# Weight loads in 4,096-byte pieces, rounding in place, and a third group of prepared weights in a fused attention, gated and leaky feed-forward kernel

## The chip, the cores and the metric

One core of a Trainium2 chip runs the whole program. The metric is the device time of one execution in microseconds (us). The kernel before has a median of 1567.53 us over 3 runs (1563.97 to 1570.9). The execution that the profiler recorded took 1571.51 us, 1569.7 us of it from the first to the last instruction.

## The reference, cut to what matters

```python
def sm_attn(qq, kk, vv):
    s = scale * np.matmul(qq, kk.transpose(0, 1, 3, 2))
    s = s - np.max(s, axis=-1, keepdims=True)
    a = np.exp(s)
    return np.matmul(a / (np.sum(a, axis=-1, keepdims=True) + 1e-09), vv)
p_packed = sm_attn(p, k, v)             # 32 packed rows per head
out = sm_attn(q, p_packed, p_packed)    # 8 batches, 8 heads, 576 tokens, 64 wide
x = out.transpose(0, 2, 1, 3).reshape(4608, 512)
x = (1 / (1 + np.exp(-(x @ w_gate))) * (x @ w_val)) @ w_out     # 512 -> 1536 -> 512
h = x @ w_in                                                    # 512 -> 2048
return (np.maximum(0.01 * h, h) @ w_out2).astype(np.float32)    # 2048 -> 512
```

The five weight matrices are float64 (8 bytes a number); q, k, v and p are float32.

## The kernel before, in words

The work has two stages that share the core's memory one after the other.

**The gated stage** goes batch by batch (8 batches of 576 tokens). `attention(b)` makes the two softmaxes of a batch. The second one has only 32 packed rows to look at, so the kernel never forms the attention output: for each group `i` of 256 gate and 256 value columns, `m_mm(i)` (L653) multiplies the packed rows by the weights into a small matrix. ScalarE (ACT) casts it to a high part `mh` and VectorE (DVE) takes the low part `ml` (L673, L676). `mm(f, g)` (L681) then multiplies `mh` and `ml` by the softmax `Ah`, `Al` for gate (g = 0) and value (g = 1) of 128 columns, ACT takes the sigmoid (`sg`, L702), DVE multiplies (L708), and the result is stored to `g1d` in device memory (L713). A batch has 6 groups `i` and 12 blocks `f`, the stage 96 sigmoids.

**The second stage** (`block`, L759) computes the three plain matrix products for 768 tokens at a time with a seven-product scheme (L852). It reads the gated result back (`rawg`, L925) and prepared weights (`wu`, L767).

**Weights.** `unit` (L217) turns 512 float64 numbers per partition into float32, rounded. A load takes both 32-bit words of each number into `raw64` (4 buffers). `scale` (ACT, L228) and `shift` and `sign` (DVE, L235, L239) build the float32 from the high word in a tile `cvs`; `low` (ACT, L231) makes the correction from the low word in `cvf`; `total` (GpSimd, POOL, L247) adds the two into the target. There are 24 units for gate and value weights, which go to the tiles `wc` and stay there, and 44 for the second stage. `staged` (L280) puts 2 units into a tile `Y`, forms the seven combinations (DVE, L311), splits them into high and low parts in `HL` (ACT L317, POOL L323) and stores them (L331) in device memory. There are 22 such groups, with 2 tiles `Y` and 2 tiles `HL`.

**Order.** All of this is a list of tasks with an engine, an assumed cost, a rank, the tasks that must come first, and places taken from pools of buffers. `Plan.run` (L55) simulates the list and writes the instructions in the order that it finds; each engine then runs its own instructions strictly in that order. The queue of the sync engine (SP) issues nearly all loads and the `g1d` stores, POOL issues the stores of prepared weights and the `rawg` loads.

**Handover.** The left memory of the gated stage (`raw64`, `Y`, `HL` and so on) is given up in `open_left`, which stands behind every unit and every stored group (L1059). The right memory (`sg`, `Ah`, `wc` and so on) is given up in `open_right`, which stands behind the last DVE product of the gated stage (L1060); that task also issues the last `g1d` store. `rawg` and `wu` tiles lie on the left, operand tiles `op` on the right:

```python
opened_left = add("", 0, 0, open_left, sum([*stored.values(), *units], []))
opened_right = add("", 0, 0, open_right, [glu_end[B - 1]])
```

Of the kernel before, what the change touches and what calls it, by code (L numbers as in the profile page):

```python
# [17 lines left out]
P = 128  # L18
# [114 lines left out]
def pack_attention_glu_lrelu(  # L133
# [67 lines left out]
    wc = [early.tile([P, NJ, 2, 256], F32, name=f"wc{i}") for i in range(NF1 // 2)]  # L201
# [12 lines left out]
    for name, n in (("raw64", 4), ("cv", 3), ("Y", 2), ("HL", 2)):  # L214
        plan.pool(name, n)

    def unit(key, rank, load, target, after=(), give=(), loads=1):  # L217

        t = {}

        def do_load():
            t["raw"] = stage.tile([P, 512, 2], I32, tag="raw64", bufs=4, name="raw64")
            load(t["raw"])

        def scale():
            t["s"] = stage.tile([P, 512], F32, tag="cvs", bufs=3, name="cvs")
            t["f"] = stage.tile([P, 512], I32, tag="cvf", bufs=3, name="cvf")
            nc.scalar.activation(t["s"], t["raw"][:, :, 1].bitcast(F32), AF.Copy, scale=2.0 ** -112)  # L228

        def low():  # L230
            nc.scalar.activation(t["f"], t["raw"][:, :, 0].bitcast(U32), AF.Copy, scale=2.0 ** -29)  # L231

        def shift():
            s = t["s"].bitcast(I32)
            nc.vector.tensor_single_scalar(s, s, 3, op=ALU.logical_shift_left)  # L235

        def sign():
            s = t["s"].bitcast(I32)
            nc.vector.scalar_tensor_tensor(  # L239
                out=s, in0=t["raw"][:, :, 1], scalar=-(1 << 31), in1=s,  # L240
                op0=ALU.bitwise_and, op1=ALU.bitwise_or,
            )

        def total():
            x = target().bitcast(I32)
            n = x.shape[1]
            nc.gpsimd.tensor_tensor(  # L247
                out=x,
                in0=t["s"].bitcast(I32).rearrange("p (a b) -> p a b", a=n),
                in1=t["f"].rearrange("p (a b) -> p a b", a=n),  # L250
                op=ALU.add,
            )
# [27 lines left out]
    def staged(st, g, kk, rank):  # L280
# [365 lines left out]
    def gated(b, units):  # L646
# [6 lines left out]
        def m_mm(i):  # L653
            def fn():
                ps = ps_pair()
                for j in range(NJ):
                    for hh in range(2):
# [4 lines left out]
                            wc[i][r, j].rearrange("p g c -> p (g c)"),  # L662
# [54 lines left out]
        for i in range(NF1 // 2):  # L717
            m = add("PE", 1.2, r0 + 16 * i - 95, m_mm(i), [packed[b], *units[i]], take=[K("misc", i), K("mhl", i)],
# [322 lines left out]
    with tc.manual_schedule():  # L1041
# [5 lines left out]
        units = [[unit_gv(i, g, jh) for g in range(2) for jh in range(2)] for i in range(NF1 // 2)]  # L1047
# [45 lines left out]
```

## Time and profile before

| | us |
|---|---|
| median of 3 runs (lowest, highest) | 1567.53 (1563.97, 1570.9) |
| the profiled execution | 1571.51 |
| its span, first to last instruction | 1569.7 |
| TensorE (PE) busy | 1426.4 (91%) |
| VectorE (DVE) busy | 1082.0 (69%) |
| ScalarE (ACT) busy | 768.0 (49%) |
| GpSimd (POOL) busy | 437.7 (28%) |
| all 16 DMA engines, hardware queue | 67.3% of the span |

Times in the profile count from the first instruction. In rows, `out<-in` names the tile written and the tiles read, L and a number is a line of the kernel, and what stands behind `<-` in square brackets or after "waited for" is what ended an engine's wait. PE is the engine to watch: where it is idle, the end of the program moves.

### The profile page before, as it was taken

Reading aid. Unit: us, or ns where it says so; the run is one execution under the profiler, and the core shown is the slowest. Engines: PE = TensorE matmul, PEld = TensorE weight load, DVE = VectorE, ACT = ScalarE, POOL = GpSimd, SP = SyncE. Lnnn points to the kernel's source line nnn. Section 1 sums busy time; section 2 is a strip of 40 time slices with the busy share of each in tenths; the row PEclk is TensorE's granted clock in tenths of the full one; section 3 lists DMA queues with packets and bytes.
Section 4 is the critical chain, followed back from the end, with each engine's and each line's share of the span. In section 5 each row is a group of like instructions: output and inputs, shape, how many; then the busy total and the mean of one; then the engine's idle time right before and its main releaser. Section 6 shows DMA issues by size and latency. Waiting matters only on the chain.

```text
span 1569.7 us, 26707 instructions
## 1 busy us (share of the span) xinstructions
PE 1426.4 (91%) x10368; PEld 1336.0 (85%) x10368; DVE 1082.0 (69%) x1438; ACT 768.0 (49%) x1017; POOL 437.7 (28%) x514
## 2 busy tenths in 40 slices
PE   4687989998889828999999999999999999999995
PEld 1565777876768718999999999999999999999995
DVE  5787878967877627668566865687558755885491
ACT  4476666756565524454345433554355434543450
POOL 1332343314345652001710160026001620130006
PEclk8898999999999959999999999999999999999998
DMA  9994686776566879888998899889988898898884
GB/s 227 255 249 153 224 302 221 251 248 213 189 232 228 293 272 355 295 253 264 324 331 254 261 336 320 252 263 319 334 253 264 288 364 257 256 290 253 253 255 120
DMA packets 143070, 414.92 MB, mean 264 GB/s; under 512 B 24544, under 2 KB 35552, under 8 KB 142944
## 3 DMA queue, kind: packets, MB, share of 16 engines
q1 hardware_dynamic: 115744, 335.07, 67.3%
q0 software_dynamic: 27200, 78.14, 14.5%
q8 instruction: 83, 1.36, 0.4%
q14 instruction: 43, 0.35, 0.1%
HBM read 335.02 MB, written 78.12 MB: 263 GB/s over the span
## 4 chain that ended last, share of the span: by engine, by line
PE 70%; DMA 12%; DVE 7%; ACT 4%; POOL 3%; issue 3%; SPq 0%; POOLq 0%; ACTq 0%; DVEq 0%
PE ps_pair L852 60%; PE ps_pair L692 8%; DMA wd<-HL 2%; DMA raw<-in_moe_w_gate_dram 2%; DMA raw<-in_moe_w_out_dram 2%; DMA wu<-HL 1%; DVE Y L311 1%; DMA v<-in_v_dram 1%; POOL out_dram L1027 1%; POOL HL L323 1%; DVE ml L676 1%; DMA rawg<-g1d 1%; PE ps_pair L659 1%; POOL Y L247 1%; DVE cvs L235 1%
## 5 line engine op out<-in xcount | busy, mean ns | idle before, releaser
L852 PE MATMUL ps_pair<-op,wu 128*128 128x384 f32 x5544 | 965.7, 337 | 39.5 <-DMA wu<-wp 33.5
L852 PEld LDWEIGHTS ps_pair<-op,wu 128*128 128x128 f32 x5544 | 963.6, 189 | 41.5 <-ACT op L795 33.5
L1027 POOL DMA_DIRECT2D out_dram<-os x256 | 150.3, 595 | 618.8 <-DVE os L1014 609.5
L795 ACT CAST op<-rawg 128x768 fp32r<-128x768 f32 x168 | 138.3, 835 | 245.3 <-DVE rawg L786 121.3
L692 PE MATMUL ps_pair<-Ah,ml 128*128 128x288 f32 x768 | 181.1, 318 | 52.8 <-DVE ml L676 22.5
L800 DVE TENSOR_TENSOR op<-rawg,op 128x768 fp32r<-128x768 f32 x168 | 158.3, 951 | 87.3 <-ACT op L795 86.1
L692 PEld LDWEIGHTS ps_pair<-Ah,ml 128*128 128x128 f32 x768 | 126.9, 197 | 101.9 <-ACT sg L702 27.6
L869 DVE TENSOR_TENSOR tmp<-ps_pair,tmp 128x768 f32<-128x768 f32 x72 | 68.8, 956 | 154.4 <-PE ps_pair L852 106.0
L692 PE MATMUL ps_pair<-Al,mh 128*128 128x288 f32 x768 | 169.9, 303 | 0.3 <-DVE Al L581 0.2
L692 PE MATMUL ps_pair<-Ah,mh 128*128 128x288 f32 x768 | 169.0, 302 | 0.0
L795 ACT CAST op<-G 128x768 fp32r<-128x768 f32 x168 | 134.7, 834 | 59.8 <-PE ps_pair L852 44.8
L800 DVE TENSOR_TENSOR op<-G,op 128x768 fp32r<-128x768 f32 x168 | 155.7, 948 | 7.7 <-ACT op L795 7.3
L323 POOL TENSOR_TENSOR HL<-Y,HL 128x1024 fp32r<-128x1024 f32 (+1 forms) x44 | 94.7, 2155 | 129.7 <-ACT HL L317 128.3
L692 PEld LDWEIGHTS ps_pair<-Al,mh 128*128 128x128 f32 x768 | 128.6, 196 | 0.9 <-DVE Al L581 0.9
L692 PEld LDWEIGHTS ps_pair<-Ah,mh 128*128 128x128 f32 x768 | 127.8, 195 | 0.0
L925 POOL DMA_DIRECT2D rawg<-g1d x96 | 68.0, 712 | 160.7 <-ACT op L795 66.6
L988 ACT ACTIVATE G<-G 128x768 f32<-128x768 f32 x96 | 81.2, 846 | 59.0 <-DVE G L985 58.0
L247 POOL TENSOR_TENSOR Y<-cvs,cvf 128x512 int32<-128x512 int32 x44 | 58.5, 1334 | 149.2 <-DVE cvs L239 104.8
L863 ACT COPY tmp<-ps_pair 128x768 f32<-128x768 f32 x72 | 57.5, 799 | 84.5 <-PE ps_pair L852 84.0
L786 DVE TENSOR_TENSOR rawg<-rawg 128x768 f32<-128x768 f32 x96 | 90.2, 952 | 4.1 <-DMA rawg<-g1d 3.3
L786 DVE TENSOR_TENSOR G<-G 128x768 f32<-128x768 f32 x96 | 91.1, 950 | 0.3
L708 DVE TENSOR_TENSOR sg<-sg,ps_pair 128x576 f32<-128x576 f32 x96 | 71.5, 744 | 28.0 <-ACT sg L702 11.2
(75 smaller groups left out, 1147.3 us busy)
## 6 DMA issues: line engine op xcount, KB each, us to landing
wu<-wu SPq DMA_DIRECT2D x168, 512.0 KB, 4.6
wu<-wd SPq DMA_DIRECT2D x168, 512.0 KB, 4.5
wu<-wp SPq DMA_DIRECT2D x126, 512.0 KB, 5.0
g1d<-sg SPq DMA_DIRECT2D x96, 288.0 KB, 4.0
rawg<-g1d POOLq DMA_DIRECT2D x48, 384.0 KB, 8.7
raw<-in_moe_w_out_dram SPq DMA_DIRECT2D x28, 512.0 KB, 6.8
raw<-in_k_dram SPq DMA_DIRECT2D x16, 576.0 KB, 5.1
raw<-in_q_dram SPq DMA_DIRECT2D x16, 576.0 KB, 6.2
```

The lines of the kernel that those rows point to most:

```text
L247: nc.gpsimd.tensor_tensor(out=x, in0=t["s"].bitcast(I32).rearrange("p (a b) -> p a b", a=n), in1=t["f"].rearrange("p (a b) -> p a b", a=n) ...
L323: nc.gpsimd.tensor_tensor(out=hl[:, :, 1], in0=t["y"][:, x0:x1], in1=hl[:, :, 0].bitcast(F32), op=ALU.subtract,)
L692: nc.tensor.matmul(ps[:, t, :HS], w, x[:, t * HS:(t + 1) * HS], start=(n == 0), stop=(n == len(pairs) - 1),)
L708: nc.vector.tensor_tensor(out=sg, in0=sg, in1=st["gv", f, 1][:, :, :HS], op=ALU.mult)
L786: nc.vector.tensor_tensor(out=src(g, o), in0=src(g, a), in1=src(g, b), op=ALU.subtract)
L795: nc.scalar.copy(h, src(g, c))
L800: (nc.gpsimd if on_pool(i, g) else nc.vector).tensor_tensor(out=l, in0=src(g, c), in1=tiles["op", st, i, g][0].bitcast(F32), op=ALU.subtract)
L852: nc.tensor.matmul(ps[c][:, m, :TB], a, x[:, kk, :], start=(fresh and kk == 0 and y == 0), stop=(end and kk == 1 and y == 2), skip_group_c ...
L869: nc.vector.tensor_tensor(out=T[x], in0=ps[c][:, :, :TB], in1=T[y], op=ALU.add)
L925: nc.gpsimd.dma_start(out=t[:, :, t0 - base:t0 - base + m], in_=g1d[b][:, f:f + 2, s0:s0 + m])
L988: nc.scalar.activation(dest(), dest(), AF.Prelu, alpha=0.01)
L1027: nc.gpsimd.dma_start(out=ob[:, s0:s0 + m, d0:d0 + 32], in_=tiles["os", c][32 * y:32 * y + 32, x, t0:t0 + m],)
```

## The change

It has five parts:

- a gate or value unit is now 512 neighbouring columns of one pair of 64-row strips, instead of 256 columns of two pairs: each row that a load reads is one run of 4,096 bytes, before it was two of 2,048. One `wc` tile now holds what two held, and two groups `i` need the same 8 units, before each needed 4 of its own;
- `scale`, `shift` and `sign` work in the target (`wc` or `Y`) itself, and `total` adds `cvf` into it; `cvs` is gone;
- a third `Y` tile;
- a staged unit's load no longer stands behind a free `Y`; its `scale` does;
- the planner's assumed costs of `shift` and `sign` are 0.6 and 0.78 instead of 0.42 and 0.75.

```diff
-    wc = [early.tile([P, NJ, 2, 256], F32, name=f"wc{i}") for i in range(NF1 // 2)]
+    wc = [early.tile([P, NJ, 2, 512], F32, name=f"wc{i}") for i in range(NF1 // 4)]
...
-    for name, n in (("raw64", 4), ("cv", 3), ("Y", 2), ("HL", 2)):
+    for name, n in (("raw64", 4), ("cv", 3), ("Y", 3), ("HL", 2)):
...
         def scale():
-            t["s"] = stage.tile([P, 512], F32, tag="cvs", bufs=3, name="cvs")
+            x = t["x"] = target()
+            nc.scalar.activation(
+                x, t["raw"][:, :, 1].bitcast(F32).rearrange("p (a b) -> p a b", a=x.shape[1]),
+                AF.Copy, scale=2.0 ** -112,
+            )
...
-        L = add("DMA", 1.7, rank, do_load, after, take=[("raw64", ("raw64", key))])
-        a = add("ACT", act(512), rank, scale, [L], take=[("cv", ("cv", key))])
-        c = add("ACT", act(512), rank, low, [a], give=[("raw64", key)])
-        s = add("DVE", 0.42, rank, shift, [a])
-        s = add("DVE", 0.75, rank, sign, [s], give=[("raw64", key)])
-        return add("POOL", gps(512), rank, total, [c, s, *after], give=[("cv", key), *give])
+        L = add("DMA", 1.7, rank, do_load, take=[("raw64", ("raw64", key))])
+        a = add("ACT", act(512), rank, scale, [L, *after])
+        c = add("ACT", act(512), rank, low, [a], take=[("cv", ("cv", key))], give=[("raw64", key)])
+        s = add("DVE", 0.6, rank, shift, [a])
+        s = add("DVE", 0.78, rank, sign, [s], give=[("raw64", key)])
+        return add("POOL", gps(512), rank, total, [c, s], give=[("cv", key), *give])
...
-                r0 = (hh * NJ + 2 * jh) * D
+                r0 = (hh * NJ + j) * D
                 nc.sync.dma_start(
-                    out=raw[64 * hh:64 * hh + 64].rearrange("p (j c) b -> p j (c b)", j=2),
-                    in_=w[r0:r0 + 2 * D, i * 512:(i + 1) * 512].rearrange("(j d) c -> d j c", d=D),
+                    out=raw[64 * hh:64 * hh + 64].rearrange("p c b -> p (c b)"),
+                    in_=w[r0:r0 + D, i * 1024:(i + 1) * 1024],
                 )
...
-            ("gv", i, g, jh), -60 + 4 * i + 2 * g + jh, load,
-            lambda: wc[i][:, 2 * jh:2 * jh + 2, g],
+            ("gv", i, g, j), -60 + 8 * i + 2 * j + g, load, lambda: wc[i][:, j:j + 1, g],
...
-                            wc[i][r, j].rearrange("p g c -> p (g c)"),
+                            wc[i // 2][r, j, :, (i % 2) * 256:(i % 2 + 1) * 256],
...
-            m = add("PE", 1.2, r0 + 16 * i - 95, m_mm(i), [packed[b], *units[i]], take=[K("misc", i), K("mhl", i)],
+            m = add("PE", 1.2, r0 + 16 * i - 95, m_mm(i), [packed[b], *units[i // 2]], take=[K("misc", i), K("mhl", i)],
```

The planner makes another order of it. **First place: ACT at the end of the gated stage**, where `sg` are the last sigmoids, `HL` the casts of prepared weights, `cvs`, `cvf` and `Y<-raw` the rounding of staged units, `op` the first cast of the second stage. Before:

```order
L702 ACTIVATE sg<-ps_pair 128x576 x2
L317 CAST HL<-Y 128x4x256
L317 CAST HL<-Y 128x3x256
L228 ACTIVATE cvs<-raw_6287 128x512
L231 ACTIVATE cvf<-raw_6287 128x512
L228 ACTIVATE cvs<-raw_6298 128x512
L231 ACTIVATE cvf<-raw_6298 128x512
L317 CAST HL<-Y 128x4x256
L317 CAST HL<-Y 128x3x256
L795 CAST op<-rawg 128x768 x11
```

Now:

```order
L315 CAST HL<-Y 128x3x256
L700 ACTIVATE sg<-ps_pair 128x576
L671 CAST mh<-ps_pair 128x1024
L700 ACTIVATE sg<-ps_pair 128x576 x2
L671 CAST mh<-ps_pair 128x1024
L700 ACTIVATE sg<-ps_pair 128x576 x2
L671 CAST mh<-ps_pair 128x1024
L700 ACTIVATE sg<-ps_pair 128x576 x2
L671 CAST mh<-ps_pair 128x1024
L700 ACTIVATE sg<-ps_pair 128x576 x3
L793 CAST op<-rawg 128x768 x6
```

Before, two units and four `HL` casts stand behind the last sigmoid; now the last `HL` cast stands ahead of the last ten sigmoids. **Second place: SP around the same point**, where `raw` are the last loads of staged units, `g1d` the stores of the gated stage, `wu` the first loads of the second stage. Before:

```order
L713 DMA g1d_64<-sg 128x576
L288 DMA raw_6166<-in_moe_w_out_dram 128x1024
L713 DMA g1d_64<-sg 128x576 x3
L288 DMA raw_6287<-in_moe_w_out_dram 128x1024
L713 DMA g1d_64<-sg 128x576
L288 DMA raw_6298<-in_moe_w_out_dram 128x1024
L767 DMA wu<-wp_65 128x1024
```

Now:

```order
L286 DMA raw_5676<-in_moe_w_out_dram 128x1024
L711 DMA g1d_63<-sg 128x576 x4
L711 DMA g1d_64<-sg 128x576 x7
L765 DMA wu<-wp_65 128x1024
L711 DMA g1d_64<-sg 128x576
L765 DMA wu<-wp_66 128x1024
L711 DMA g1d_64<-sg 128x576
L765 DMA wu<-wp_67 128x1024
```

Before, the last staged load stands behind the last `g1d` store and ahead of the first `wu` load; now it stands 16 `g1d` stores ahead of the end, and `wu` loads stand between the last stores. **Third place: ACT at the first group of batch 0**, where `cvs` or `wc` and `cvf` with a `raw` number are the two ACT steps of one gate or value unit, and `w`, `Ah` belong to the second softmax. Before (the fifth to seventh unit are in these rows):

```order
L228 ACTIVATE cvs<-raw_283 128x512
L231 ACTIVATE cvf<-raw_283 128x512
L228 ACTIVATE cvs<-raw_297 128x512
L231 ACTIVATE cvf<-raw_297 128x512
L228 ACTIVATE cvs<-raw_308 128x512
L673 CAST mh<-ps_pair 128x1024
```

Now (the ninth and tenth unit are `raw_410` and `raw_418`):

```order
L577 CAST Ah<-w_389 128x2x288
L577 CAST Ah<-w_393 128x2x288
L234 ACTIVATE cvf<-raw_365 128x512
L227 ACTIVATE wc_94<-raw_410 128x512
L234 ACTIVATE cvf<-raw_410 128x512
L227 ACTIVATE wc_94<-raw_418 128x512
L234 ACTIVATE cvf<-raw_418 128x512
L671 CAST mh<-ps_pair 128x1024 x2
```

The first `mh` cast stood behind seven units and ahead of `Ah`; now two `mh` casts stand together behind ten units and behind `Ah`.

## Rows read from the trace of the kernel before

**Rows 1.** Busy time by stretch; columns are named in the first line.

```profile
core 0: us, PE busy (x) PEld busy (x) DVE busy (x) ACT busy (x) POOL busy (x), PEclk, DMA share, GB/s
44.10:129.30 85.20, 62.65 (x622) 49.62 (x622) 64.47 (x109) 54.55 (x81) 30.17 (x22) 0.86 0.87 226
129.30:546.90 417.60, 381.41 (x3967) 315.47 (x3967) 329.74 (x536) 260.39 (x363) 168.36 (x119) 0.96 0.71 237
...
620.00:1569.70 949.70, 931.67 (x5372) 930.59 (x5370) 624.09 (x697) 409.45 (x509) 199.90 (x326) 0.99 0.86 278
```

**Rows 2.** Chain that ended last, 430 to 600 us: start, us, what.

```profile
565.42 4.71 DMA wd<-HL
...
572.69 6.29 DMA rawg<-g1d
```

**Rows 3.** Timeline at the handover: start, us, engine, line, operation, [idle before <-releaser].

```profile
547.01 0.75 DVE L708 TENSOR_TENSOR sg<-sg,ps_pair 128x576 f32<-128x576 f32 x1 [0.30 <-issue]
...
547.79 0.32 SPq L713 DMA_DIRECT2D g1d<-sg  x1
...
579.28 0.83 ACT L795 CAST op<-rawg 128x768 fp32r<-128x768 f32 x1 [16.77 <-DMA rawg<-g1d]
...
580.16 0.69 PE L852 MATMUL ps_pair<-op,wu 128*128 128x384 f32 x1 [33.25 <-DMA wu<-wp]
...
581.16 7.78 PE L852 MATMUL ps_pair<-op,wu 128*128 128x384 f32 x36 [0.30 <-DVE op L800]
...
591.32 18.83 PE L852 MATMUL ps_pair<-op,wu 128*128 128x384 f32 x107 [2.38 <-DVE op L800]
```

**Rows 4.** Timeline of ACT: the tenth sigmoid from the end, and the last.

```profile
506.13 0.65 ACT L702 ACTIVATE sg<-ps_pair 128x576 f32<-128x576 f32 x1 [1.77 <-PE ps_pair L692]
...
545.36 0.65 ACT L702 ACTIVATE sg<-ps_pair 128x576 f32<-128x576 f32 x1 [2.52 <-PE ps_pair L692]
```

**Rows 5.** The `g1d` stores (L713), 500 to 560 us.

```profile
DMA to landing us min/median/max: 2.7/4.1/6.0
```

**Rows 6.** The `rawg` loads (L925), 540 to 700 us: issue ns, and landing.

```profile
L925 POOL DMA_DIRECT2D rawg<-g1d x30: 704/712/721, 572.7 to 642.6; - x30
...
DMA to landing us min/median/max: 5.3/8.5/12.5
```

**Rows 7.** Timeline of PE in batch 0: first products of groups 1 and 3.

```profile
62.19 0.85 PE L692 MATMUL ps_pair<-Ah,ml 128*128 128x288 f32 x2 [8.22 <-DVE ml L676]
...
89.20 0.53 PE L692 MATMUL ps_pair<-Ah,ml 128*128 128x288 f32 x2 [2.04 <-DVE ml L676]
```

**Rows 8.** Timeline, all engines, start of the gated stage.

```profile
36.18 1.00 ACT L673 CAST mh<-ps_pair 128x1024 fp32r<-128x1024 f32 x1
...
37.47 1.22 DVE L676 TENSOR_TENSOR ml<-ps_pair,mh 128x1024 fp32r<-128x1024 f32 x1
...
44.19 1.42 DVE L581 TENSOR_TENSOR Al<-w,Ah 128x576 fp32r<-128x576 f32 x2
...
48.78 0.66 ACT L228 ACTIVATE cvs<-raw 128x512 f32<-128x512 f32 x1
```

**Rows 9.** DMA, 46 to 97 us: queue, packets, MB, share; issues with median landing.

```profile
q1 hardware_dynamic: 6597, 13.16, 102.1%
...
raw<-in_moe_w_gate_dram SPq DMA_DIRECT2D x14, 256.0 KB, 7.3
```

**Rows 10.** DMA, 120 to 548 us.

```profile
q1 hardware_dynamic: 31932, 63.14, 45.1%
```

**Rows 11.** What ACT waited for, 120 to 548 us: total, times, longest.

```profile
ACT HL L317 <- DVE Y L311: 25.8, 16, 3.6
...
ACT cvs L228 <- DMA raw<-in_moe_w_in_dram: 7.3, 4, 4.6
```

**Rows 12.** Groups of instructions: count, busy us, mean ns.

```profile
L239 DVE SCALAR_TENSOR_TENSOR cvs<-raw,cvs 128x512 int32<-128x512 int32 x68 | 52.6, 783 | 0.9
L235 DVE TENSOR_SCALAR cvs<-cvs 128x512 int32<-128x512 int32 x68 | 42.8, 639 | 27.8 <-ACT cvs L228 27.7
```

More of the change, by code (lines that the diff above doesn't have):

```diff
@@ L225, in scale, with low @@
         def scale():
-            t["s"] = stage.tile([P, 512], F32, tag="cvs", bufs=3, name="cvs")
+            x = t["x"] = target()
[3 more added lines that the diff above has]
+            )
+        def low():
             t["f"] = stage.tile([P, 512], I32, tag="cvf", bufs=3, name="cvf")
-            nc.scalar.activation(t["s"], t["raw"][:, :, 1].bitcast(F32), AF.Copy, scale=2.0 ** -112)
@@ L230, in low @@
-        def low():
             nc.scalar.activation(t["f"], t["raw"][:, :, 0].bitcast(U32), AF.Copy, scale=2.0 ** -29)
         def shift():
-            s = t["s"].bitcast(I32)
-            nc.vector.tensor_single_scalar(s, s, 3, op=ALU.logical_shift_left)
+            x = t["x"].bitcast(I32)
+            nc.vector.tensor_single_scalar(x, x, 3, op=ALU.logical_shift_left)
         def sign():
-            s = t["s"].bitcast(I32)
+            x = t["x"].bitcast(I32)
             nc.vector.scalar_tensor_tensor(
-                out=s, in0=t["raw"][:, :, 1], scalar=-(1 << 31), in1=s,
-                op0=ALU.bitwise_and, op1=ALU.bitwise_or,
+                out=x, in0=t["raw"][:, :, 1].rearrange("p (a b) -> p a b", a=x.shape[1]),
+                scalar=-(1 << 31), in1=x, op0=ALU.bitwise_and, op1=ALU.bitwise_or,
@@ L242, in sign @@
             )
         def total():
-            x = target().bitcast(I32)
-            n = x.shape[1]
+            x = t["x"].bitcast(I32)
             nc.gpsimd.tensor_tensor(
[L248 to L251, printed above, removed]
-            )
-        L = add("DMA", 1.7, rank, do_load, after, take=[("raw64", ("raw64", key))])
-        a = add("ACT", act(512), rank, scale, [L], take=[("cv", ("cv", key))])
@@ L256, in unit @@
-        c = add("ACT", act(512), rank, low, [a], give=[("raw64", key)])
-        s = add("DVE", 0.42, rank, shift, [a])
-        s = add("DVE", 0.75, rank, sign, [s], give=[("raw64", key)])
-        return add("POOL", gps(512), rank, total, [c, s, *after], give=[("cv", key), *give])
-    def unit_gv(i, g, jh):
+                out=x, in0=x, in1=t["f"].rearrange("p (a b) -> p a b", a=x.shape[1]), op=ALU.add
+            )
+        L = add("DMA", 1.7, rank, do_load, take=[("raw64", ("raw64", key))])
@@ L262, in unit_gv @@
+        a = add("ACT", act(512), rank, scale, [L, *after])
[3 more added lines that the diff above has]
+        return add("POOL", gps(512), rank, total, [c, s], give=[("cv", key), *give])
+    def unit_gv(i, g, j):
         w = (w_gate, w_val)[g]
@@ L302, in fn @@
                 if "y" not in t:
-                    t["y"] = stage.tile([P, 8, 256], F32, tag="Y", bufs=2, name="Y")
+                    t["y"] = stage.tile([P, 8, 256], F32, tag="Y", bufs=3, name="Y")
                 return t["y"][:, 0:2] if half else t["y"][:, 6:8]
@@ L1045, in pack_attention_glu_lrelu @@
         nc.scalar.activation(tiny[1], tiny[0], AF.Exp)
-        units = [[unit_gv(i, g, jh) for g in range(2) for jh in range(2)] for i in range(NF1 // 2)]
+        units = [[unit_gv(i, g, j) for g in range(2) for j in range(NJ)] for i in range(NF1 // 4)]
         attention(0)
```

## The prediction, made before the changed kernel ran

> **What bounds the kernel now.** I read the busy times by stretch first [rows 1]. From 620 us on PE is busy 931.67 of 949.7 us: nothing can be won there except by taking matmuls away, and the change takes none. The gated stage is less full: from 129.3 to 546.9 us PE is idle 417.60 - 381.41 = 36.2 us, from 44.1 to 129.3 us 85.20 - 62.65 = 22.5 us, and before 44.1 us it has hardly anything to do. Next I followed the chain that ended last through the handover [rows 2]: it runs over the last store of prepared weights (issued at 565.42 us) to the first `rawg` load (572.69 us). The gated stage had ended long before. The timeline shows the price [rows 3]: the last DVE product starts at 547.01 us, right behind the last gated matmul (546.9 us, the edge of the stretches in rows 1), and the first matmul of the second stage starts at 580.16 us after 33.25 us without work; another 2.38 us go at 591.32 us. So the largest hole in PE's work is there because the preparation of weights ends some 23 us after the stage beside which it runs, and because the first loads follow it (6.29 us for the first, rows 2). That is the place to look at.
>
> **The handover.** The change gives preparation a third `Y`, lets its loads run ahead, and the new order shows what comes of it: the last `HL` cast stands ahead of ten sigmoids, where two units and four casts stood behind all of them. Each engine keeps its order, so this holds on the chip whatever things cost. The tenth sigmoid from the end starts at 506.13 us and the last at 545.36 us [rows 4], so the last cast is at least 40.8 us ahead of the end of the stage (546.9 - 506.1). Behind it come the low part and store, some 10 us (an estimate: 7.3 us from the last store to the first `rawg` load in rows 2, and some 3 for the low part), 18 issues of `rawg` at 0.712 us, 12.8 us, and 8.5 us to land [rows 6]: 31 us. That is 9.5 us less than there is, so loads are no longer the wait. What is late next is the right memory: the first operand cast writes where `sg` tiles lay, and so waits for the last `g1d` store. From rows: the DVE product ends at 547.76, the store is issued at 547.79 [rows 3], lands 4.1 us later [rows 5], the cast takes 0.83 us [rows 3]: PE begins at 552.7, 5.8 us after the last gated matmul. The hole shrinks by 33.3 - 5.8 = 27.5 us. Bounds: without a wait for the store it is 547.76 + 0.83, a hole of 1.7 us and a gain of 31.6; if the store lands as late as the slowest load of rows 6, 12.5 us, the hole is 14.2 and the gain 19. I take the median landing, since `wu` and `rawg` are then through for the most part.
>
> Behind the hole 2.38 us of waiting for late `rawg` go, and the first 36 matmuls, which took 7.78 us at a granted clock that the idle time had let fall, take 36 x 931.67/5372 = 6.2 us if it stays up [rows 1, 3]. Together 3.9 us; bounds 0 (the clock falls in a short hole too) and 7.1 (all 5.5 us that PE is idle from 581.2 to 620 less matmul time, by the same view).
>
> **The start.** Here the change takes something. Group 0 needs 8 units where it needed 4. The new ACT order puts the first two `mh` casts behind the tenth unit's two steps. That unit's load waits for a free `raw64`, which an earlier unit gives up when its `sign` is done, and that stands on DVE behind the whole second softmax of batch 0. DVE ended that softmax (`Al`) at 45.6 us [rows 8]. From there: two `sign` and a `shift`, 0.78 + 0.64 + 0.78 [rows 12], 47.8 us; the load 7.3 us [rows 9], 55.1; two ACT steps of 0.66, one `mh` cast of 1.00, one `ml` of 1.22 [rows 8], 58.6 us. The first gated product started at 44.1 us, the edge of a stretch in rows 1; it will start about 14 us later. (Before, `mh` of group 0 was ready at 37 us and the softmax was the last to come; now the softmax waits for the weights.) In return groups 0 and 1 are ready together, and later 2 and 3, 4 and 5: the long waits for `ml` in batch 0, 8.22 and 2.04 us [rows 7], 10 us in all, were ahead of groups 1 and 3, the second of their pairs. I take 14 - 10 = +4 us. Bounds: +14, when nothing is won back, and 14 - 22.5 = -8.5, when all of PE's idle time in that stretch goes.
>
> That lower end would need the longer pieces. From 46 to 97 us the hardware queue kept its 16 engines busy at 102.1% and moved 13.16 MB, most of it weights in runs of 2,048 bytes [rows 9]: 13.16/(51 x 16 x 1.021) = 15.8 KB per engine and us. From 120 to 548 us, with more runs of 4,096, it moved 63.14/(428 x 16 x 0.451) = 20.4 [rows 10]. The 12.6 MB of gate and value weights would take 12.6/(16 x 0.0158) = 50 us before and 38.5 now: 11 us less of queue time. Little of it reaches PE: by the order above loads wait for buffers, not for the queue. The Trainium skill speaks against even these 11 us: its page "DMA: Bandwidth & Descriptors", section "Specifications", wants 512 bytes for line rate and no more. By that rule the term is 0. The two rates do not agree with it, though the stretches differ in more than the length of a run.
>
> **The middle.** Operations stay the same: five per unit, the same shapes, DVE 0.64 and 0.78 us [rows 12]; working in place removes a tile, not an instruction, and I cost it at 0 (below: nothing; above: rival 4). But 22 groups that were spread from about the eleventh sigmoid to beyond the 96th now end by the 86th: 13% denser, which on 36.2 us of idle time is +5 us; and the last ten blocks are free of them, where 40 us of the stage ran at the same idle share, -3.5 us. Loads that run ahead of `Y` spare ACT waits such as the 7.3 us for `w_in` [rows 11], of which PE sees a part, say -1.5. Sum 0. Bounds -15 (ACT's 25.8 us of waiting for `Y` [rows 11] goes too and half of it reaches PE) and +36 (idle time doubles).
>
> **Sum.** -27.5 - 3.9 + 4 + 0 = -27.4 us against the profiled execution, 1571.5 - 27.4 = 1544.1. That execution lies 4.0 us above the median of the three runs (1571.51 - 1567.53), so the forecast on their scale is 1540 us. What a measurement of this kernel can't tell from no change is about 0.5%, 7.8 us: 1559.7 to 1575.4 us.
>
> **The rivals.**
> 1. *The late start is paid in full.* The pair of groups waits for its second half each time, and batch 0 ends 14 us later: 10 us more than in the sum, 1550 us. For it: in the new order SP's loads 11 to 16 each need a `sign` that stands between other DVE work. Against: batch 0 has 22.5 us of slack in PE.
> 2. *The start and the middle win.* Faster pieces take the -8.5 instead of +4 at the start, and loads ahead of `Y` 2 us in the middle: 1540 - 12.5 - 2 = 1525.5 us. For it: 102.1% of the queue. Against: loads that wait for buffers.
> 3. *The change does not end the preparation early.* If stores or the low parts on POOL lag by the 9.5 us to spare and 27.5 more, the hole stays: 1540 + 27.5 = 1567.5 us, no change. For it: `HL` has two tiles as before. Against: the order of ACT, which can't slip behind ten sigmoids.
> 4. *DVE is crowded: slower.* With three groups in flight a `shift` and a `sign` stand ahead of `ml` where none stood. DVE is busy 329.74 of 417.60 us [rows 1]. Batches 1 to 7 have 42 groups `i`; 0.64 + 0.78 = 1.42 us ahead of each is 60 us on PE: 1600 us. It decides from 35.4 us on (1575.4 - 1540), 0.84 us for each `ml`. Against: the groups are ranked behind all gated work, and a step goes first only when the planner finds DVE free.
>
> **How the numbers follow.** The forecast has 0.60 (its own range 1529 to 1551: the bounds of the handover's landing and half of those of start and middle), rival 1 0.15, rival 2 0.14, rival 3 0.06, rival 4 0.05. The first three are faster: 0.89. Rival 3 is no change: 0.06. Rival 4 is slower: 0.05. The range 1521 to 1558 leaves out rivals 3 and 4 and the far end of rival 2.
>
> **What would show it.** Right: in the changed profile PE is idle 4 to 9 us between the last product of L690 and the first of L850, what ends it is the first cast or the last store and not `wu` or `rawg`, and the first `rawg` issue stands 25 to 35 us ahead of the last sigmoid. The first gated product stands at 55 to 60 us, batch 0 has fewer waits for `ml`, and PE's idle time from there to the end of the stage is 30 to 42 us. The second stage from its first matmul on is 3 to 7 us shorter. Wrong: a hole above 15 us (the handover), a first product before 50 us (the start), or idle time above 60 us in batches 1 to 7 (the middle).

## The result and the profile after

The changed kernel takes 1548.72 us, median of 4 runs (1546.39 to 1551.92), against 1568.99 us for 4 runs of the kernel before: ratio 0.9878, 95% interval 0.9857 to 0.9900. The forecast was 1540 us with a range of 1521 to 1558. The profiled execution took 1550.15 us, 1548.3 us of it span.

The span is 21.4 us shorter than before. It can be cut at three places that both traces show: the end of batch 1's last sigmoid, the last gated matmul, and the first matmul of the second stage.

| stretch | before, us | after, us | difference | forecast |
|---|---|---|---|---|
| to the end of batch 1 | 189.7 | 190.2 | +0.5 | +4 (start) |
| batches 2 to 7, to the last gated matmul | 357.2 | 370.3 | +13.1 | 0 (middle) |
| hole | 33.3 | 4.9 | -28.4 | -27.5 |
| second stage from its first matmul | 989.6 | 982.9 | -6.7 | -3.9 |

(Lines of the changed kernel: sigmoid L700, `ml` L674, gated products L690, DVE product L706, `sign` L242, `shift` L238, combinations L309, cast L315, low part L321, `total` L249, second stage L850. All but those of `unit` are 2 lower than before.)

**The handover.** Timeline of the changed kernel, as in [rows 3]: start, us, engine, line, operation, and the idle time before it with what ended it.

```profile
532.99 10.18 POOL L923 DMA_DIRECT2D rawg<-g1d  x14 [4.12 <-DMA g1d<-sg]
...
558.89 0.65 ACT L700 ACTIVATE sg<-ps_pair 128x576 f32<-128x576 f32 x1 [2.55 <-PE ps_pair L690]
...
560.55 0.76 DVE L706 TENSOR_TENSOR sg<-sg,ps_pair 128x576 f32<-128x576 f32 x1 [2.44 <-PE ps_pair L690]
561.33 0.32 SPq L711 DMA_DIRECT2D g1d<-sg  x1
...
564.55 1.56 ACT L793 CAST op<-rawg 128x768 fp32r<-128x768 f32 x2 [5.01 <-DMA g1d<-sg]
...
565.44 0.69 PE L850 MATMUL ps_pair<-op,wu 128*128 128x384 f32 x1 [4.98 <-ACT op L793]
...
566.43 33.81 PE L850 MATMUL ps_pair<-op,wu 128*128 128x384 f32 x181 [0.31 <-DVE op L798]
```

The `rawg` loads begin 26 us ahead of the last sigmoid. What the first cast waits for is the last `g1d` store, and PE begins 4.98 us after it stopped, not 33.25. The second wait, 2.38 us in [rows 3], is gone: 181 matmuls follow without a break.

**The middle.** Busy times of the changed kernel for batches 2 to 7, and for the second stage from 40 us after its first matmul; columns as in [rows 1].

```profile
190.20:560.50 370.30, 328.13 (x3379) 267.46 (x3363) 320.21 (x464) 229.25 (x320) 181.68 (x137) 0.97 0.77 263
...
605.00:1548.30 943.30, 925.00 (x5335) 924.23 (x5333) 623.32 (x696) 409.45 (x509) 200.01 (x326) 0.99 0.86 280
```

The same of the kernel before, batches 2 to 7:

```profile
189.70:546.90 357.20, 327.33 (x3383) 270.21 (x3383) 279.68 (x452) 222.13 (x311) 150.82 (x107) 0.96 0.71 239
```

PE has the same work (327.33 and 328.13 us); its idle time goes from 29.9 to 42.2 us. DVE is busy 40.5 us longer. The longest rows of what PE waited for in these batches (total, times, longest), before:

```profile
PE ps_pair L483 <- ACT w L475: 12.6, 4, 5.5
PE ps_pair L692 <- DVE ml L676: 10.8, 8, 2.9
PE ps_pair L692 <- ACT sg L702: 7.0, 4, 2.6
```

and after:

```profile
PE ps_pair L690 <- DVE ml L674: 10.9, 8, 3.2
PE ps_pair L426 <- DVE sg L706: 7.7, 3, 3.0
PE ps_pair L502 <- DVE sg L706: 4.8, 1, 4.8
PE ps_pair L690 <- ACT sg L700: 4.3, 6, 1.3
PE ps_pair L481 <- ACT w L473: 4.1, 3, 1.7
...
```

Summed over all rows of the view, PE waited 12.2 us for DVE and 20.0 for ACT before, 33.5 and 8.4 after. So of the 12.3 us that PE is idle longer the rows name 9.7: 21.3 more for DVE, in part made up by 11.6 fewer for ACT. DVE by groups of instructions (count, busy us, mean ns) says what kept it; before:

```profile
L708 DVE TENSOR_TENSOR sg<-sg,ps_pair 128x576 f32<-128x576 f32 x72 | 53.6, 744 | 21.8 <-PE ps_pair L692 8.6 <-ACT sg L702 8.6 <-issue 2.6
L311 DVE TENSOR_TENSOR Y<-Y 128x256 f32<-128x256 f32 x74 | 46.0, 652 | 7.9 <-POOL Y L247 7.1
L239 DVE SCALAR_TENSOR_TENSOR cvs<-raw,cvs 128x512 int32<-128x512 int32 x35 | 27.4, 791 | 0.6
L235 DVE TENSOR_SCALAR cvs<-cvs 128x512 int32<-128x512 int32 x34 | 21.9, 656 | 8.5 <-ACT cvs L228 8.5
```

after:

```profile
L309 DVE TENSOR_TENSOR Y<-Y 128x256 f32<-128x256 f32 x78 | 60.3, 796 | 0.7
L706 DVE TENSOR_TENSOR sg<-sg,ps_pair 128x576 f32<-128x576 f32 x72 | 53.5, 743 | 17.5 <-ACT sg L700 10.3 <-PE ps_pair L690 6.4 <-issue 0.5
L242 DVE SCALAR_TENSOR_TENSOR Y<-raw,Y 128x512 int32<-128x512 int32 x38 | 43.1, 1138 | 0.3
L238 DVE TENSOR_SCALAR Y<-Y 128x512 int32<-128x512 int32 x37 | 30.0, 823 | 0.0
```

The products, which read PSUM (`ps_pair`), take what they took. The three groups that read and write tiles in the core's memory are each longer per instruction: 38 x (1138 - 791) + 78 x (796 - 652) + 37 x (823 - 656) ns = 30.6 us of the 40.5; most of the rest is that a few more of them fall into this stretch. One of them at close range, in the timeline of the changed kernel:

```profile
456.14 4.77 POOL L321 TENSOR_TENSOR HL<-Y,HL 128x1024 fp32r<-128x1024 f32 x2
...
456.39 2.86 DVE L242 SCALAR_TENSOR_TENSOR Y<-raw,Y 128x512 int32<-128x512 int32 x1
...
459.17 2.03 DVE L238 TENSOR_SCALAR Y<-Y 128x512 int32<-128x512 int32 x1
...
461.12 0.74 DVE L706 TENSOR_TENSOR sg<-sg,ps_pair 128x576 f32<-128x576 f32 x1
...
461.92 1.34 PE L502 MATMUL ps_pair<-v,aT 128*32 128x64 f32 x36 [4.82 <-DVE sg L706]
```

A `sign` and a `shift`, whose medians over the stage are 0.68 and 0.42 us, take 2.86 and 2.03 us beside two low parts of GpSimd; the product behind them is late, and PE stands 4.82 us. The Trainium skill, "SBUF — State Buffer", section "Who interferes with whom", has this: a DVE instruction with two SBUF inputs, or one in a two-port mode, uses a port pair that it shares with GpSimd, and the one that issues later is blocked until the other instruction is done. The trace agrees here: the longest `sign` (2.86 us) is its own 0.68 and about one low part (2.2 us on the mean), and the instructions on PSUM keep their times.

### The profile page after: what moved, and what is told of

It reads as the page before. It is cut to its first block, busy times and chain, and to the rows that moved or that the text cites. A ratio compares the mean times of both kernels' runs of the same rounds, so it can differ in the third digit from the quotient of the medians.

```text
span 1548.3 us, 26643 instructions
## 1 busy us (share of the span) xinstructions
PE 1428.3 (92%) x10368; PEld 1331.0 (86%) x10368; DVE 1117.1 (72%) x1438; ACT 768.1 (50%) x1019; POOL 439.9 (28%) x514
## 3 DMA queue, kind: packets, MB, share of 16 engines
q0 software_dynamic: 27200, 78.14, 14.4%
## 4 chain that ended last, share of the span: by engine, by line
PE 75%; DVE 11%; DMA 5%; ACT 4%; issue 3%; POOL 1%; SPq 0%; POOLq 0%; DVEq 0%; ACTq 0%
PE ps_pair L850 61%; PE ps_pair L690 10%; DVE Y L309 2%; DMA raw<-in_moe_w_val_dram 2%; DMA raw<-in_moe_w_gate_dram 2%; DVE Y L242 2%; DVE sg L706 1%; DVE Y L238 1%; PE ps_pair L657 1%; DVE ml L674 1%; PE ps_pair L426 1%; DMA raw<-in_q_dram 1%; POOL out_dram L1025 1%; ACT L700 1%; DMA wu<-wp 1%
## 5 line engine op out<-in xcount | busy, mean ns | idle before, releaser
L850 PE MATMUL ps_pair<-op,wu 128*128 128x384 f32 x5544 | 964.3, 337 | 5.7 <-ACT op L793 5.0
L850 PEld LDWEIGHTS ps_pair<-op,wu 128*128 128x128 f32 x5544 | 963.1, 188 | 6.7 <-ACT op L793 5.2
L690 PE MATMUL ps_pair<-Ah,ml 128*128 128x288 f32 x768 | 176.4, 312 | 30.5 <-DVE ml L674 22.1
L690 PEld LDWEIGHTS ps_pair<-Ah,ml 128*128 128x128 f32 x768 | 124.4, 193 | 76.8 <-ACT sg L700 23.5
L690 PE MATMUL ps_pair<-Ah,mh 128*128 128x288 f32 x768 | 167.4, 300 | 0.0
L690 PE MATMUL ps_pair<-Al,mh 128*128 128x288 f32 x768 | 167.0, 300 | 0.0
L321 POOL TENSOR_TENSOR HL<-Y,HL 128x1024 fp32r<-128x1024 f32 (+1 forms) x44 | 96.6, 2204 | 110.2 <-ACT HL L315 98.9
L690 PEld LDWEIGHTS ps_pair<-Ah,mh 128*128 128x128 f32 x768 | 126.4, 193 | 0.0
L690 PEld LDWEIGHTS ps_pair<-Al,mh 128*128 128x128 f32 x768 | 126.2, 193 | 0.0
L249 POOL TENSOR_TENSOR Y<-Y,cvf 128x512 int32<-128x512 int32 x44 | 58.7, 1340 | 119.3 <-DVE Y L242 110.0
L700 ACT ACTIVATE sg<-ps_pair 128x576 f32<-128x576 f32 x96 | 62.0, 648 | 60.1 <-PE ps_pair L690 56.4
```

Of the source, the lines that this page charges most:

```text
L249: nc.gpsimd.tensor_tensor(out=x, in0=x, in1=t["f"].rearrange("p (a b) -> p a b", a=x.shape[1]), op=ALU.add)
L321: nc.gpsimd.tensor_tensor(out=hl[:, :, 1], in0=t["y"][:, x0:x1], in1=hl[:, :, 0].bitcast(F32), op=ALU.subtract,)
L690: nc.tensor.matmul(ps[:, t, :HS], w, x[:, t * HS:(t + 1) * HS], start=(n == 0), stop=(n == len(pairs) - 1),)
L700: nc.scalar.activation(st["sg", f], st["gv", f, 0][:, :, :HS], AF.Sigmoid)
L850: nc.tensor.matmul(ps[c][:, m, :TB], a, x[:, kk, :], start=(fresh and kk == 0 and y == 0), stop=(end and kk == 1 and y == 2), skip_group_c ...
```

## The experiments

The theories by their letters in the expectations: **C**, DVE's instructions wait behind GpSimd's and are late for PE; **S**, the late start is carried through to the end; **L**, the chain of a group counts in its whole length, GpSimd's part of it too; **D**, the memory of the third group is worth more elsewhere. What came of all runs, as differences to the kernel before in the stretches of the first table (profiled executions), and what PE waited in batches 2 to 7:

| run | time, us (ratio, 95%) | to end of batch 1 | batches 2 to 7 | hole | second stage | PE waits for DVE / ACT |
|---|---|---|---|---|---|---|
| before | - | 189.7 | 357.2 | 33.3 | 989.6 | 12.2 / 20.0 |
| changed | 1548.7 (0.9857-0.9900) | +0.5 | +13.1 | -28.4 | -6.7 | 33.5 / 8.4 |
| e12, changed again | 1544.2 (0.9820-0.9886) | -5.8 | +13.3 | -29.1 | -7.7 | 31.3 / 8.1 |
| e1, old loads | 1557.3 (0.9890-0.9947) | +8.7 | +11.1 | -29.3 | -7.4 | 29.4 / 10.9 |
| e2, new loads alone | 1560.9 (0.9932-0.9962) | -5.6 | -13.8 | +10.5 | -2.8 | 18.0 / 6.2 |
| e3, two groups | 1543.3 (0.9818-0.9855) | -7.2 | +9.4 | -23.2 | -8.0 | 24.2 / 16.4 |
| e11, e3 again | 1544.2 (0.9821-0.9868) | -8.3 | +11.3 | -24.5 | -6.9 | 25.1 / 16.7 |
| e10, e3, loads wait | 1582.6 (1.0055-1.0117) | -7.0 | -3.3 | +24.7 | -3.0 | 7.3 / 23.4 |
| e9, e3, third HL | 1540.6 (0.9798-0.9845) | -6.3 | +6.5 | -22.7 | -8.8 | 22.2 / 14.4 |
| e4, small low parts | 1507.2 (0.9588-0.9620) | -11.5 | -18.1 | -29.0 | -6.6 | 4.0 / 16.9 |
| e5, low parts cut in 256 | 1547.2 (0.9839-0.9893) | -4.4 | +16.8 | -28.7 | -7.1 | 20.6 / 20.6 |
| e6, GpSimd cut in 128 | 1565.0 (0.9963-0.9987) | -5.8 | +35.0 | -28.7 | -7.9 | 28.9 / 26.8 |
| e7, e3, cut in 256 | 1548.7 (0.9854-0.9906) | -1.7 | +14.1 | -22.6 | -7.9 | 19.6 / 22.6 |
| e8, e7, `sg` stays | 1549.2 (0.9847-0.9896) | -6.9 | +11.0 | -23.5 | -8.5 | 20.0 / 21.9 |

(In e2 and e10 the last sigmoid comes 3 to 4 us behind the last gated matmul: ACT stands ahead of it in a cast that waits for a store, 4.88 us in e2. The time from that matmul on counts as hole.)

The stretches are not waits alone. In batches 2 to 7 PE is busy 327.33 us before, 328.13 in the changed kernel, 320.21 in e2, 318.12 in e4 and 336.24 in e6, with nearly the same count of matmuls and a mean granted clock of 0.96, 0.97, 0.99, 0.99 and 0.93: some 7 of e2's 13.8 us, 10 of the 31.2 between e4 and the changed kernel, and 9 of e6's 35 go with the clock, not with waits.

### Which part of the change does what

**e1**: the changed kernel with the gate and value loads of before.

```diff
-                r0 = (hh * NJ + j) * D
+                r0 = (hh * NJ + 2 * jh) * D
...
-                    in_=w[r0:r0 + D, i * 1024:(i + 1) * 1024],
+                    in_=w[r0:r0 + 2 * D, i * 512:(i + 1) * 512].rearrange("(j d) c -> d j c", d=D),
```

> The changed kernel with gate and value weights loaded as before (pieces of 2,048 bytes, four units for each group i); rounding in place, the third Y and loads ahead of Y stay. In its order the last HL cast stands still further ahead of the end of the gated stage. Theory C (the gated stage ends 13.5 us later because DVE instructions take longer while GpSimd works beside them): the first gated product is back at 44 us, but the stage still ends 8 us or more later than before (555 us or later), the hole at the handover is 5 us, the time 1543 to 1553 us. Theory S (the late start is carried through all batches): the stage ends at 547 us and the time is 1533 to 1538 us.

1557.28 us, 4 us above what C said. The first gated product is back at 47.7 us (64.6 in the changed kernel), and yet batch 1 ends 8 us later than there, and the stage ends at 566.7 us. S falls: the late start is not what costs.

**e2**: the kernel before with the new gate and value loads (the diff of e1 the other way round), nothing else.

> The kernel before with the new gate and value loads alone (pieces of 4,096 bytes, eight units for two groups i). Theory C: the first gated product at 60 to 65 us as in the changed kernel, but by the end of batch 1 nothing of that is left, the stage ends within 4 us of 547 us, the hole stays (30 us or more): 1563 to 1573 us. Theory S: the stage ends 13 us later and the time is 1580 to 1585 us.

1560.93 us, better than either theory said: these loads alone gain 7.9 us, and the rest alone (e1) 11.6 against the 1568.86 us of before on that chip; together 19.5, and the change as a whole gained 20.3. Within the spread the parts add. The loads gain 5.6 us by the end of batch 1, though the first gated product comes at 60.7 us, and 13.8 in batches 2 to 7; 10.5 of that goes again into a longer hole, 43.8 us, at whose end a `wu` load stands.

**e3**: the changed kernel with two tiles `Y`.

```diff
-    for name, n in (("raw64", 4), ("cv", 3), ("Y", 3), ("HL", 2)):
+    for name, n in (("raw64", 4), ("cv", 3), ("Y", 2), ("HL", 2)):
...
-                    t["y"] = stage.tile([P, 8, 256], F32, tag="Y", bufs=3, name="Y")
+                    t["y"] = stage.tile([P, 8, 256], F32, tag="Y", bufs=2, name="Y")
```

> The changed kernel with two tiles Y instead of three. In its order the preparation ends 4 products ahead of the end of the gated stage, with three tiles 15. Theory C: less work of GpSimd beside DVE at a time, so sign and shift are shorter than in the changed kernel (mean of sign under 0.95 us, there 0.99) and the stage ends at 550 to 558 us; the hole is 12 to 25 us, for the rawg loads come late: 1553 to 1563 us. Theory S: the stage ends at 560 us as in the changed kernel, 1560 to 1572 us.

**e11, e12**: e3 and the changed kernel again, on one chip.

> The changed kernel with two groups instead of three once more, beside the changed kernel itself on one chip. If a third group costs what the first run of this said (1543.3 against 1548.7, from runs on two chips), this is 3 to 8 us shorter than the changed kernel beside it; if it was the chip, the two are within 2 us.

> The changed kernel as it is, beside the three others on one chip: 1546 to 1552, 0.986 to 0.990 of the kernel before.

Neither theory had e3's 1543.30 us (1553 or more) or its hole of 10.1 us (12 to 25); the mean `sign` of batches 1 to 7 is shorter, as C said (0.91 us against 1.10). e3 seemed 5 us faster than the changed kernel; side by side the two have 1544.24 and 1544.20 us (the changed kernel 2 us below what was expected of it). All 8 runs of each have medians of 1543.7 and 1546.8. So the third group, which stands in the title, is worth nothing that these runs can show: it takes 4 to 6 us off the hole, and the stage ends 4 to 11 us later (560.5 and 554.4 against 549.1 and 549.9 us).

**e10**: e3 with loads that wait for a free `Y`, as before the change.

```diff
-        L = add("DMA", 1.7, rank, do_load, take=[("raw64", ("raw64", key))])
+        L = add("DMA", 1.7, rank, do_load, after, take=[("raw64", ("raw64", key))])
```

> The changed kernel with two groups in flight, and its loads of the expert weights wait for a free group as before the change: left of the change are the gate and value loads in 4 KB pieces and the rounding in place. It stands between the kernel before with the new gate and value loads (1561) and the changed kernel with two groups (1543). If the loads ahead of the group are what gives the 17 us between them, the time is 1556 to 1563 and the start of the second stage again waits more than 15 us for a prepared weight; if the rounding in place gives it, 1543 to 1549, and the hole is the 10 us of two groups with early loads.

1582.59 us, 38 more than e11: slower than the kernel before. Its hole and its POOL from the end of the stage on (groups: count, busy us, mean ns):

```profile
PE ps_pair L850 <- DMA wu<-wp: 58.0, 1, 58.0
```

```profile
L249 POOL TENSOR_TENSOR Y<-Y,cvf 128x512 int32<-128x512 int32 x6 | 7.7, 1290 | 1.0 <-DVE Y L242 0.9
```

Six units, three groups, are rounded after the stage. The size is beyond both expectations, the side is that of the loads: letting them run ahead of `Y` is the part of the change that closes the hole. Rounding in place alone does not: e10 differs from e2 by that and the planner's costs, and takes 21.7 us more (on another chip). Why three groups are left here, and two in e2, was not followed up, and loads ahead of `Y` without rounding in place were not tried.

**e9**: e3 with a third `HL`.

```diff
-    for name, n in (("raw64", 4), ("cv", 3), ("Y", 3), ("HL", 2)):
+    for name, n in (("raw64", 4), ("cv", 3), ("Y", 2), ("HL", 3)):
...
-                hl = t[x0] = stage.tile([P, 4, 2, 256], F32R, tag="HL", bufs=2, name="HL")
+                hl = t[x0] = stage.tile([P, 4, 2, 256], F32R, tag="HL", bufs=3, name="HL")
```

> The changed kernel with two groups (Y) in flight, as before the change, and a third pair of cast parts (HL) instead, so that a cast no longer waits for the store of the pair two before it. Theory D (where the memory of the third group was better spent): in the run with two groups ScalarE waited 29.5 us in the stage for such stores (wd, wu and wp from HL); most of them go, the stage ends 5 to 12 us earlier than its 549, and the time is 1531 to 1540. Theory C (the stage pays for each instruction of VectorE and GpSimd that is put into it, and the waits of ScalarE only shift it): a denser preparation again makes the gated products late, the stage ends at 549 to 558, and the time is 1543 to 1552, no better than two groups alone.

1540.55 us (1538.85 to 1542.22): the best version here that does the whole work. Its four runs lie below all of e11 and e12 on that chip; the intervals of the ratios still overlap. What ACT waited in e11 from 129 to 545 us

```profile
ACT HL L315 <- DVE Y L309: 26.8, 14, 5.8
ACT HL L315 <- DMA wp<-HL: 10.3, 4, 5.3
ACT HL L315 <- DMA wu<-HL: 10.2, 6, 3.9
ACT HL L315 <- DMA wd<-HL: 7.7, 3, 4.1
```

is in e9

```profile
ACT HL L315 <- DVE Y L309: 34.8, 20, 3.7
...
ACT HL L315 <- DMA wd<-HL: 1.7, 1, 1.7
```

The waits for stores go, 28.2 to 1.7 us, as D says, but 8 us come back as waits for DVE, and the stage ends 2.8 us earlier, not 5 to 12. The size of D was wrong, and C's 1543 to 1552 too.

### Why the middle is longer

**e4**: GpSimd's low parts on 8 columns only (the two `HL` tiles are made once, and their low halves set to zero at the start).

```diff
-                    out=hl[:, :, 1], in0=t["y"][:, x0:x1], in1=hl[:, :, 0].bitcast(F32),
+                    out=hl[:, :1, 1, :8], in0=t["y"][:, x0:x0 + 1, :8], in1=hl[:, :1, 0, :8].bitcast(F32),
```

> The changed kernel, in which GpSimd's subtraction that makes the low parts of the prepared weights works on 8 columns of one combination instead of on all (the rest of the low parts stays zero, so the products of the second stage lack the low part of the weights); the order of all instructions is the same. Theory C: with 95 us of GpSimd's work gone, DVE's combinations, signs and shifts take what they take alone for the most part (mean of the combinations below 0.55 us, now 0.76; of sign below 0.85), DVE is busy at least 25 us less in the gated stage, which ends 8 to 15 us earlier (546 to 553 us); time 1534 to 1542 us. Theory S or a theory of the order alone (the same instructions wait for the same others): the stage ends within 4 us of 560 us.

1507.16 us, 41.6 less than the changed kernel. DVE, and PE's waits, in batches 1 to 7:

```profile
L245 DVE SCALAR_TENSOR_TENSOR Y<-raw,Y 128x512 int32<-128x512 int32 x44 | 33.7, 771 | 0.3
L241 DVE TENSOR_SCALAR Y<-Y 128x512 int32<-128x512 int32 x44 | 27.5, 638 | 0.1
```

```profile
PE ps_pair L694 <- DVE ml L678: 1.7, 2, 1.6
```

`sign` is down to 771 ns, `shift` to 638, and of PE's waits for DVE 4.0 of 33.5 us are left. So GpSimd's low parts are what makes DVE late; whether by their length each or by their time in all, e4 does not tell. The gain is nearly three times the most that C said (1534 to 1542 us, 7 to 15 us less), so more than DVE's longer instructions may hang on the low parts.

**e5, e6**: the same work of GpSimd in shorter instructions: low parts of 256 columns (e5), low parts and `total` of 128 (e6). The low parts of e6; e5 has 256 in place of 128:

```diff
-                nc.gpsimd.tensor_tensor(
-                    out=hl[:, :, 1], in0=t["y"][:, x0:x1], in1=hl[:, :, 0].bitcast(F32),
...
+                for x in range(x1 - x0):
+                    for c in range(0, 256, 128):
+                        nc.gpsimd.tensor_tensor(
+                            out=hl[:, x, 1, c:c + 128], in0=t["y"][:, x0 + x, c:c + 128],
```

> The changed kernel, in which each GpSimd subtraction for the low parts (1,024 or 768 columns, 2.4 or 1.8 us) is cut into pieces of 256 columns; the result and the order of everything else are the same, GpSimd is busy as long or somewhat longer. Theory C (DVE instructions that read or write memory on two ports wait until the GpSimd instruction beside them ends): a wait is at most one piece, some 0.6 us, so the mean of the combinations falls from 0.76 us to 0.45 to 0.60 us, DVE is busy 15 to 35 us less in the gated stage, and the stage ends 8 us or more earlier: 1525 to 1542 us. Theory L (what the kernel with nearly no low parts won it won because the chain of one group became shorter): the chain is no shorter here, so the time stays at 1546 to 1556 us.

> As the run before, with pieces of 128 columns for the low parts, and GpSimd's additions of the rounding (512 columns, 1.3 us) cut into pieces of 128 as well. Theory C: waits of DVE are at most 0.35 us or so, mean of the combinations below 0.5 us and of sign below 0.8 us; but GpSimd pays for four times as many instructions, which lengthens the chain of a group: 1518 to 1542 us. Theory L: 1550 us or more.

e5 1547.19 us, as the changed kernel; e6 1564.95, 16 us more. In e5 PE waits 12.9 us less for DVE than in the changed kernel and 12.2 us more for ACT. In e6, groups of batches 1 to 7, then what ACT waited for in batches 2 to 7:

```profile
L325 POOL TENSOR_TENSOR HL<-Y,HL 128x128 fp32r<-128x128 f32 x308 | 152.6, 528 | 81.8 <-ACT HL L317 80.3 <-issue 1.5
...
L242 DVE SCALAR_TENSOR_TENSOR Y<-raw,Y 128x512 int32<-128x512 int32 x44 | 34.4, 787 | 0.3
L238 DVE TENSOR_SCALAR Y<-Y 128x512 int32<-128x512 int32 x44 | 27.2, 632 | 3.4 <-ACT Y L227 3.4
```

```profile
ACT HL L317 <- DMA wu<-HL: 28.3, 7, 6.5
ACT Y L227 <- POOL HL L325: 24.6, 8, 6.1
ACT HL L317 <- DMA wp<-HL: 17.7, 3, 10.6
```

DVE's instructions are on the mean as short as in e4 (787 and 632 ns), yet PE waits 28.9 us for DVE and 26.8 for ACT. The low parts take 152.6 us instead of 96.6 and `total` 85.0 instead of 58.7, so `Y` and `HL` come free late, ACT's casts and scalings stand waiting for them, and sigmoids and `mh` casts stand behind those. Not all of it is that: PE's two longest waits for DVE, 6.7 and 6.5 us, stand behind a `shift` of 4.82 us and a combination of 3.11 us, each beside a row of `total` pieces. C in its pure form (only DVE's longer instructions) falls, and L's side stands: each engine keeps its order, and what holds up a step of the preparation holds up the gated work written behind it. How the middle's 13 us divide between the two was not measured.

**e7, e8**: e3 with low parts and `total` in pieces of 256; in e8 also with `sg` in memory that the handover does not use. The part of e8 alone:

```diff
+    sgs = [lowest.tile([P, 2, NT // B // 2], F32, name=f"sg{x}") for x in range(3)]
...
-                st["sg", f] = early.tile([P, 2, HS], F32, tag="sg", bufs=3, name="sg")
+                st["sg", f] = sgs[(b * NF1 + f) % 3]
```

> The changed kernel with two tiles Y, and both GpSimd instructions cut into pieces of 256 columns. Theory C: the gain over two tiles Y alone (1543 us) is the gain of cutting in the run with three tiles, somewhat less since fewer waits are there: 1522 to 1538 us. Theory L: 1540 to 1550 us.

> As the run before, with the three sg tiles in memory that is not handed over, so that the first operand cast does not wait for the last g1d store to land. The hole at the handover was 5.0 us in the changed kernel and ended with that store; without the wait it is 1.7 to 3 us if the rawg loads and weights are there: 2 to 4 us less than the run before. If wu or rawg loads end the hole, as with two tiles Y (10 us, ended by wu), it stays as in the run before.

1548.65 and 1549.24 us, both some 5 us above e3, as L said; the intervals touch. Short pieces give nothing here either, though DVE's instructions are short (the longest `sign` takes 1.51 us, 2.87 in e3): PE waits 4.6 us less for DVE than in e3 and 6.2 us more for ACT. Where `sg` lies makes no difference while loads (`rawg` in e7, `wu` in e8), not the last store, end the hole (10.7 and 9.8 us).

## Why the prediction was right, and where not

**The handover** was right in mechanism and size: 4.9 us instead of 5.8, ended by the first cast behind the last store, with `rawg` begun 26 us ahead of the last sigmoid (25 to 35 foretold). The store landed in 3.0 us where the median of [rows 5] was taken. e10 and e3 show what carried it: the loads ahead of `Y`; the third `Y` is worth the last 4 to 6 us of it.

**The second stage** gained 6.7 instead of 3.9. Of 5544 matmuls, 5372 were left 40 us after the first one before [rows 1], 5335 now: 37 x 0.173 us = 6.4. The upper bound, 7.1, was the better value, but one of the term's two parts did not come. The first matmuls were to be faster because the clock stays up; they are no faster. Before and after, columns as in [rows 1]:

```profile
581.10:589.00 7.90, 7.78 (x36) 7.46 (x36) 3.83 (x5) 2.52 (x4) 4.37 (x7) 0.82 1.03 365
```

```profile
566.40:574.30 7.90, 7.87 (x33) 7.87 (x34) 6.06 (x7) 2.65 (x4) 0.00 (x0) 0.70 0.30 76
```

After only 4.9 us without a matmul the granted clock was 0.70 on the mean of these 7.9 us, as the prediction's lower bound feared. What gave the time is PE's idle time in these 40 us: 5.5 us before (581.2 to 620), 0.3 now (565.4 to 605), where the sum had counted 2.38.

**The start** came out at +0.5 and, in e12, at -5.8 by the end of batch 1, inside its bounds (+14 to -8.5), but for other reasons than given. The first gated product came at 64.6 us, not 58.6:

```profile
58.53 0.66 ACT L227 ACTIVATE wc<-raw 128x512 f32<-128x512 f32 x1 [10.15 <-DMA raw<-in_moe_w_gate_dram]
...
64.58 0.85 PE L690 MATMUL ps_pair<-Ah,ml 128*128 128x288 f32 x2 [8.14 <-DVE ml L674]
```

The loads of the ninth and the tenth unit took 12 us each, where 7.3 had been taken. (The first line is the ninth's; ACT's wait for it was 7.28 us in e12, where the product came at 59.4.) What gave the time back was not the waits for `ml`, as I wrote: these stayed. PE's waits from 44 us to the end of that stretch in [rows 1], before:

```profile
PE ps_pair L692 <- ACT Ah L579: 15.7, 3, 9.0
PE ps_pair L692 <- DVE ml L676: 11.1, 3, 8.2
```

and after:

```profile
PE ps_pair L657 <- POOL wc L249: 13.8, 3, 9.4
PE ps_pair L690 <- DVE ml L674: 10.7, 2, 8.1
```

The waits for `Ah`, the second softmax, are gone: while the weights come later (13.8 us of waits for `wc`), attention gets ahead. In batch 1 another 6.8 us of them go. Rival 1 (paid in full) has the nearest number, 1550 us, but falls by e1. Within one kernel a late load may still count: the changed kernel's two profiled executions, on two chips, differ by 5.2 us at the first product and by 7.7 at the end.

**The longer pieces.** The hardware queue from 46 to 97 us, as in [rows 9], in the changed kernel and then in e1, which has the old pieces:

```profile
q1 hardware_dynamic: 3989, 11.06, 88.7%
```

```profile
q1 hardware_dynamic: 6996, 13.20, 100.2%
```

That is 11.06/(51 x 16 x 0.887) = 15.3 KB per engine and us with 4,096-byte runs, and 16.1 with 2,048. The 20.4 that I set against 15.8 came from another stretch, not from the length of the runs. The trace agrees with the rule of the Trainium skill, "DMA: Bandwidth & Descriptors", section "Specifications", that I weighed against it: the longer run brought no higher rate. That the gain of the new loads (e2) is one of order follows only by elimination.

**The middle** is the step that failed: cost 0, measured +13.1 and +13.3 in batches 2 to 7. "Operations stay the same" was true of their number and not of their time. I had reckoned density against PE's idle time and held DVE's 0.64 and 0.78 us, the means of the trace before, for what they would stay. They contain the waits beside GpSimd (from 129.3 to 546.9 us `sign` takes 651 ns at the least, 823 on the mean), and with the low parts denser `sign` takes 1138 ns on the mean of batches 2 to 7. How much of the 13 us is this, and how much that gated work stands behind a longer chain of preparation, stays open (e5 to e8). Rival 4 named the right engine: PE's waits for DVE grew by 21.3 us, about a third of its 60, but most of it is not the wait for `ml` that it named (10.8 and 14.7 us in all rows of `ml`); its 1.42 us for a `shift` and a `sign` were 4.89 in the longest case above. PE's idle time from the first gated product to the end of the stage, 30 to 42 us by the prediction, came out at 55.3 (47.0 in batches 1 to 7, where above 60 was to mean wrong). The sum said -27.4 us for the profiled execution and -21.4 came: 13.1 lost in the middle, of which the start gave back 3.5, the second stage 2.8 and the hole 0.9. So the number is as near as it is partly by luck: three smaller terms erred the other way.

## What to carry to other kernels

When preparation runs beside a stage, price it by what its instructions will take while the other engines work as densely as the new order has it, and look for instructions whose mean is far above their minimum: that mean need not stay. Shorter instructions on the engine in the way did not help where their time in all grew. What closed the hole was letting loads run ahead of the buffer in which they end; a further buffer behind them took as much in the stage as it gave in the hole. Work moved from a hole into a full stage is not free: about half of what the handover gained went that way.

## What the runs showed of the hardware that was not expected

Cutting a GpSimd instruction into shorter ones costs much: the low parts took 2.20 us each (1024 or 768 columns, 96.6 us in all), 0.842 us for 256 columns (125.0 in all), and 0.528 for 128 (152.6).

The end of one GpSimd instruction does not always free DVE. In e5 the longest `sign`, 3.52 us, lies beside two whole `total` (1.30 and 1.29 us), one right behind the other. In e6 the longest `sign` fell to 0.95 us, but the longest `shift` rose from 2.61 to 4.82 us: it lies beside nine pieces of `total` of some 0.45 us each and the issue of a store between them. In e7, with both in pieces of 256, no `sign` and no `shift` of batches 1 to 7 took more than 1.51 us. So a waiting instruction does not always get in between two pieces, which the picture of one wait for one instruction does not explain; when it does, no run here shows.
